# Masks as a PE bias, two heads per normalising instruction and constants behind the first loads, in a one-core attention and soft-MoE kernel

## The chip, the cores and the metric

The kernel runs on one core of a Trainium2 chip. The metric is device time in microseconds (us): the median of the runs before is 207.54 us (three runs: 206.69, 207.54 and 234.59).

The core has five engines with queues of their own, each in program order: PE (TensorE, matrix products into the eight PSUM banks), ACT (ScalarE), DVE (VectorE), POOL (GpSimd) and SP (SyncE). Here POOL issues all large loads, and SP issues the stores. Engines wait for one another through semaphores.

## The reference

Two steps follow each other. The first is attention over 8 batches, 8 heads, 576 tokens and a head size of 64. Heads 0 to 3 see the last 32 tokens ("plain"), heads 4 to 7 see every fourth of the last 128 ("dilated").

```
scores = scale * (q @ k.T);  rel = pos_q - pos_k
mask_plain = (rel >= 0) & (rel < 32)
mask_dil   = (rel >= 0) & (rel < 128) & (rel % 4 == 0)
attn = softmax(where(mask, scores, -1e9));  x = attn @ v      # x: 4608 tokens x 512
```

The second is a soft mixture of 8 experts with 4 slots each over these 4608 tokens:

```
logits = x @ phi                                  # 4608 x 32
slot_input = softmax(logits, over tokens).T @ x   # 32 x 512
slot_out[e] = relu(slot_input[e] @ w1[e]) @ w2[e] # w1: 512x1024, w2: 1024x512 per expert
out = softmax(logits, over slots) @ slot_out      # 4608 x 512
```

The output needs the sum over all tokens, so the experts can start only when the attention of the last batch is done, and the stores only when the experts are done.

## The kernel before, in words

Work is cut into 16 **halves** (`half(i)`, line 416): batch `i // 2` with its four plain heads (even `i`) or its four dilated heads (odd `i`). A half goes through these steps; the short names are those of the program's operations.

- **Loads** (line 304): k, q and v of the half, converted to bf16 on the way, into one of four staging slots. Between them POOL issues pieces of the expert weights (lines 314, 321, 328; 32 pieces in all); `W_AFTER` says how many pieces follow which half. The last six pieces of w2 are written over the staging slots, so they wait until the last half has been read out of them.
- **T** (line 426, DVE): three transposes of 32x32 blocks bring head size onto partitions.
- **SC** (lines 439 to 456, PE): scores in two rounds per half, one bank for each of the four heads (banks 0 to 3). **EX** (line 470, ACT): one exp over all four banks, which writes P to SBUF. The next round of scores needs the same banks, so it waits for EX. **MK** (line 475, DVE): P times a 0/1 mask.
- **TB** (line 497, PE) and **VE** (line 503, ACT): v transposed back to tokens on partitions, and copied out.
- **PV** (line 527, PE): per head, P times v and a column of ones, into one bank. **RC** and **NM** (lines 535, 539, DVE): reciprocal of the row sums, and the product with it. In dilated halves a rest of 64 tokens goes through PZ, RCz and NMz (lines 552, 560, 563).
- **XT** and **XE** (lines 579/585 PE, 595/598/602 ACT): x transposed. In dilated halves follow, for the batch, **LG** and **EXL** (lines 618, 626: logits and their exp), **ET** and **EE** (641, 647), **SI** (659, PE) and **SA** (667, DVE): the running sum of slot inputs.

After the last half come **RS** (line 741), the first expert product **L1** (705; banks zeroed before by DVE, line 711), its ReLU (715), transposes HT (725), the second product **L2** (757) in two halves of columns, then the output tiles **O** (788, PE), their scaling by ACT and DVE (797, 800) and twelve stores.

The order on each engine is written by a planner (`Sched`, line 51): it simulates the engines with the durations given to each `op` and takes, of what could start within 0.15 us, the operation with the smallest priority (`OFFS` and `PERIOD` give it). It also hands out PSUM banks: 0 to 3 belong to SC until the last EX, 4 to 7 go to every other PSUM user, one at a time. On POOL, constants (the identity, the masks; `const_ops`, line 353) have priority -90, and the loads of half `i` have -100 + `i`, weights -50.

Of the kernel before, what the change touches and what calls it, by code (L numbers as in the profile page):

```python
# [50 lines left out]
class Sched:  # L51
# [42 lines left out]

    def run(self, pool, late_banks, late_after):
# [13 lines left out]
        held = {b: [] for b in list(pool) + list(late_banks)}  # L109
        qfree = 0.0  # L110
# [8 lines left out]
        while True:  # L119
            best = None  # L120
            for e in self.ENG:
                cands = []
# [20 lines left out]
            for b in o.opens:
                i = min(banks, key=lambda k: (banks[k][0], k))
                _, rel = banks.pop(i)
                o.deps.update(rel)
# [25 lines left out]
def bass_dilated_sliding_attn__then__soft_moe_slots_kernel(  # L172
# [28 lines left out]
    VBK = 2 * 4 * 34  # L201
# [7 lines left out]
    o_sit = take(128)  # L209
# [688 lines left out]
```

## Time and profile before

| what | value |
|---|---|
| median of three runs | 207.54 us |
| the profiled execution's own time | 208.19 us |
| its span (first to last instruction) | 206.5 us |
| mean clock granted to PE | 0.759 |
| DVE busy / PE busy / ACT busy / POOL busy | 148.2 / 133.9 / 106.8 / 49.0 us |
| read from HBM / written to HBM | 61.93 MB / 9.44 MB |

The profiled execution took 1.69 us more than its span. Busy time is the time in which an engine worked on at least one instruction. The PE clock has two levels, 1.2 and 2.4 GHz, shown as 0.50 and 1.00; a value between them is a mean over a stretch. Bytes of loads are counted as written (bf16); twice as many are read (fp32).

### The profile page before, as it was taken

The page shows a single profiled execution, that of the slowest core. Times are in us where ns is not written, and L with a number is a line of the kernel's source. Part 1 is how long each engine was busy: PE and PEld are TensorE (multiplying, and loading weights), DVE is VectorE, ACT ScalarE, POOL GpSimd, SP SyncE. Part 2 cuts the span into 40 slices and gives each one's busy share as a digit, 9 for nine tenths or more (in the row PEclk, how much of TensorE's full clock was granted, in tenths as well). Part 3 has the DMA queues.
Part 4 walks back from the last instruction along what each step waited for, and adds up shares of the span by engine and source line. Part 5 has one row for each costly group of instructions (what it writes and reads, how often), then busy time and mean ns, then how long its engine had stood idle before and what let it go on. Part 6 is the DMA issues. An engine that isn't in the chain of part 4 may idle for free.

```text
span 206.5 us, 5220 instructions
## 1 busy us (share of the span) xinstructions
PE 133.9 (65%) x2139; PEld 96.4 (47%) x2140; DVE 148.2 (72%) x284; ACT 106.8 (52%) x167; POOL 49.0 (24%) x98
## 2 busy tenths in 40 slices
PE   0056649767794797688668489669626897988000
PEld 0045536655483576467556367447423535632000
DVE  6997698799779989999899998992673200299100
ACT  0065717845476747756677756774604140499000
POOL 7609904501504133232056000008000000000000
PEclk9999999755579567559987856966855569999655
DMA  5935999999999999999999999999999000099997
GB/s 82 206 68 102 208 210 214 210 212 211 213 211 213 213 210 212 214 210 210 212 214 208 215 212 216 210 213 195 183 193 156 3 5 0 3 300 360 417 421 330
DMA packets 19431, 40.77 MB, mean 197 GB/s; under 512 B 1744, under 2 KB 8912, under 8 KB 18640
## 3 DMA queue, kind: packets, MB, share of 16 engines
q0 software_dynamic: 15104, 30.94, 80.3%
q1 hardware_dynamic: 4304, 9.50, 12.1%
q8 instruction: 17, 0.28, 0.5%
q14 instruction: 6, 0.05, 0.1%
HBM read 61.93 MB, written 9.44 MB: 346 GB/s over the span
## 4 chain that ended last, share of the span: by engine, by line
DVE 45%; PE 33%; ACT 8%; issue 6%; DVEq 1%; ACTq 0%
DVE ar L426 16%; DVE ar L539 12%; PE ps L618 6%; PE ps L449 6%; DVE ar L475 5%; DVE fs L535 4%; PE ps L788 4%; ACT ar L470 3%; PE ps L705 3%; PE ps L757 3%; PE ps L527 3%; PE ps L585 2%; DVE ar L563 2%; ACT ar L797 2%; PE ps L497 2%
## 5 line engine op out<-in xcount | busy, mean ns | idle before, releaser
L426 DVE STREAM_TRANSPOSE ar<-ar 128x576 uint32<-128x576 uint32 x48 | 56.4, 1236 | 0.3 <-PE ps L456 0.3
L470 ACT ACTIVATE ar<-ps 128x1152 bf16<-128x1152 f32 (+1 forms) x32 | 37.9, 1186 | 21.4 <-PE ps L456 10.6
L539 DVE TENSOR_TENSOR ar<-ps,fs 96x384 bf16<-96x384 f32 (+1 forms) x64 | 31.3, 489 | 2.3
L503 ACT ACTIVATE ar<-ps 128x768 bf16<-128x768 bf16 x32 | 25.1, 816 | 6.2 <-PE ps L497 6.1
L475 DVE TENSOR_TENSOR ar<-ar 128x1152 bf16<-128x1152 bf16 (+1 forms) x32 | 24.6, 778 | 3.9 <-ACT ar L470 3.9
L527 PE MATMUL ps<-ar 128*128 128x66 bf16 x320 | 20.0, 230 | 8.5 <-DVE ar L475 3.0
L497 PE MATMUL ps<-ar 128*128 128x128 bf16 x192 | 20.2, 269 | 7.4 <-DVE ar L426 4.5
L527 PEld LDWEIGHTS ps<-ar 128*128 128x128 bf16 x320 | 17.2, 122 | 11.4 <-DVE ar L475 3.2
L497 PEld LDWEIGHTS ps<-ar 128*128 128x128 bf16 x192 | 15.9, 136 | 10.1 <-DVE ar L426 3.5
L535 DVE RECIPROCAL fs<-ps 96x6 f32<-96x6 f32 (+1 forms) x64 | 11.7, 183 | 12.3 <-PE ps L527 8.9
L449 PE MATMUL ps<-ar 32*128 32x128 bf16 x256 | 18.2, 412 | 3.3 <-ACT ar L470 2.0
L439 PE MATMUL ps<-ar 32*128 32x96 bf16 x384 | 9.3, 245 | 15.3 <-DVE ar L426 13.8
L800 DVE TENSOR_SCALAR ar<-ps,fs 128x256 f32<-128x256 f32 (+1 forms) x24 | 12.8, 611 | 7.4 <-PE ps L788 7.3
L618 PE MATMUL ps<-ar 128*128 128x288 bf16 x64 | 15.8, 422 | 3.0 <-ACT ar L602 3.0
L598 ACT ACTIVATE ar<-ps 128x1024 bf16<-128x1024 bf16 x8 | 8.2, 1025 | 16.1 <-PE ps L585 16.1
L304 POOL DMA_DIRECT2D ar<-in_k_dram x16 | 8.9, 554 | 28.8 <-DVE ar L426 28.0
L585 PE MATMUL ps<-ar 128*128 128x128 bf16 x80 | 9.5, 300 | 8.9 <-DVE ar L563 8.8
L439 PEld LDWEIGHTS ps<-ar 32*128 32x128 bf16 x384 | 6.4, 114 | 17.5 <-DVE ar L426 14.2
L321 POOL DMA_DIRECT2D ar<-in_moe_w_dram x12 | 6.4, 552 | 28.5 <-DVE ar L475 28.5
L304 POOL DMA_DIRECT2D ar<-in_v_dram x16 | 8.8, 548 | 17.8 <-DVE ar L426 13.2
L585 PEld LDWEIGHTS ps<-ar 128*128 128x128 bf16 x80 | 7.4, 137 | 10.5 <-DVE ar L563 10.5
L797 ACT ACTIVATE ar<-ps,fs 128x256 f32<-128x256 f32 (+1 forms) x24 | 12.1, 591 | 0.2
(63 smaller groups left out, 177.6 us busy)
## 6 DMA issues: line engine op xcount, KB each, us to landing
ar<-in_moe_w_dram POOLq DMA_DIRECT2D x32, 512.0 KB, 21.7
out_dram<-ar SPq DMA_DIRECT2D x6, 1024.0 KB, 9.7
ar<-in_k_dram POOLq DMA_DIRECT2D x16, 288.0 KB, 19.3
ar<-in_q_dram POOLq DMA_DIRECT2D x16, 288.0 KB, 19.4
ar<-in_v_dram POOLq DMA_DIRECT2D x16, 288.0 KB, 18.9
out_dram<-ar SPq DMA_DIRECT2D x6, 512.0 KB, 5.1
fs<-in_moe_phi_dram SPq DMA_DIRECT2D x1, 64.0 KB, 1.8
```

Of the source, the lines that this page charges most:

```text
L304: return pool.dma_start(a(o_stg + (s * 3 + j) * 1152, [[1, 1152]]), src[b, 4 * dl:4 * dl + 4].rearrange("h (p t) d -> (h p) (t d)", p=32))
L426: op(DVE, lambda j=j, o_dst=o_dst: dve.transpose(au(o_dst, [[1, 18], [18, 32]]), au(o_stg + (st * 3 + j) * 1152, [[32, 18], [1, 32]])), dv ...
L449: last = pe.matmul(pf(h, 128 * rr, [[1, 128]]), a(ok + 2 * res + par, [[8, 128]], 32 * h, 32), a(oq + 2 * res + par, [[8, 128]], 32 * h, 3 ...
L470: eo = op(ACT, lambda P=P, W=W: act.activation(a(P, [[W, 4], [1, W]]), AP(ps, 0, [[4096, 128], [512, 4], [1, W]]), ACTF.Exp, scale=SCALE), ...
L475: op(DVE, lambda P=P, W=W, msk=msk: dve.tensor_tensor(a(P, [[W, 4], [1, W]]), a(P, [[W, 4], [1, W]]), a(msk, [[0, 4], [1, W]]), AluOp.mult ...
L497: last = pe.transpose(pb(bank.idx, bb * 256 + par * 128, [[1, 128]]), src, a(o_id, [[1, 128]]))
L503: op(ACT, lambda t=t, bank=bank: act.activation(a(o_vb[vs] + 3 * t * VBK, [[34, 24], [1, 32]]), pb(bank.idx, 0, [[32, 24], [1, 32]]), ACTF ...
L527: last = pe.matmul(pf(bank.idx, 66 * t, [[1, 66]]), w, a(VB + t * VBK + 34 * h, [[136, 2], [1, 33]]), start=True, stop=True)
L535: op(DVE, lambda h=h, bank=bank, rows=rows: dve.reciprocal(f(rvo + 6 * h, [[1, NT]], 0, rows), pf(bank.idx, 32, [[66, NT]], 0, rows)), dve ...
L539: op(DVE, lambda h=h, bank=bank, rows=rows: dve.tensor_tensor(a(ox + 32 * h, [[256, NT], [128, 2], [1, 32]], 0, rows), pf(bank.idx, 0, [[6 ...
L585: last = pe.transpose(pb(bank.idx, 512 * par + 128 * (t % 4), [[1, 128]]), a(ox + 256 * t + 128 * par, [[1, 128]]), a(o_id, [[1, 128]]))
L618: last = pe.matmul(pf(bank.idx, 0, [[1, 288]]), a(o_phis + 128 * c, [[1, 128]]), a(o_xt[xt] + 576 * c + 288 * g, [[1, 288]]), start=(c == ...
```

## The change

1. **Masks as a bias.** MK is gone. Each round of SC begins with four products of the identity with a mask of 0 and -30000, 288 columns wide (plain) or 320 (dilated), which open each of the four banks; the score products add to it, and exp makes zeros of the masked places. SC now also waits for the masks that POOL and DVE build.
2. **Two heads per instruction.** PV writes two heads into two neighbouring banks, and one RC and one NM serve both: two of each per half in place of four, with twice the elements. The planner learns to hand out pairs of banks (`place`).
3. **V in natural order.** TB writes runs of 32 columns instead of 128, VE reads PSUM with a step and interleaves, so that PV's moving operand is 65 columns in a row and x keeps the order of d. The rows of w1 and phi are loaded in that order: w1 in two runs of 1024 per partition in place of one of 2048.
4. **Constants behind the first loads.** The first two weight pieces come before the constants on POOL, and `W_AFTER` is new: 0, 2, then 1 each, and 17 pieces after the last half.
5. **Smaller.** L1 uses 32 columns of weights per expert (zeros beyond the slots), so the zeroing of its banks goes; RS is behind `sit`; several estimated durations of the planner change.

```diff
-W_AFTER = [1, 1, 1, 2, 1, 1, 2, 1, 1, 2, 1, 1, 2, 1, 1, 13]
-PERIOD = 7.4
+W_AFTER = [0, 2, 1, 1, 1, 1, 1, 1, 1, 1, 1, 1, 1, 1, 1, 17]
+PERIOD = 6.9
...
+    def place(self, banks, opens, t):
+        left = dict(banks)
+        got = []
+        for b in opens:
+            best = None
+            for i in left:
+                idx = list(range(i, i + b.size))
+                if any(x not in left for x in idx):
+                    continue
+                key = (max([t] + [left[x][0] for x in idx]), i if b.size > 1 else -i)
+                if best is None or key < best[0]:
+                    best = (key, idx)
...
-            dma_in(fn, 128 * 1152 * 4, s_stg[s][j], -100.0 + i, f"ld{i}{'qkv'[j]}",
+            dma_in(fn, 128 * 1152 * 4, s_stg[s][j], (-100.0 if i < 2 else -80.0) + i, f"ld{i}{'qkv'[j]}",
...
-                a(o_w1 + e * 4096 + hf * 2048, [[1, 2048]]),
-                moe_w1[e, 256 * hf:256 * hf + 256, :].rearrange("(p two) f -> p (two f)", two=2))
+                a(o_w1 + e * 4096 + hf * 2048, [[1024, 2], [1, 1024]]),
+                moe_w1[e, 256 * hf:256 * hf + 256, :].rearrange("(c p) f -> p c f", p=128))
...
-            dma_in(fn, nb, sem("s_" + name), -50.0, name, writes=list(wr) + rd)
+            dma_in(fn, nb, sem("s_" + name), -100.0 if nw[0] < 3 else -80.0, name, writes=list(wr) + rd)
...
+            W, msk = (320, o_md + 320 * r) if dl else (288, o_mp + 96 * r)
+            for h in range(4):
+                pe.matmul(pf(h, 0, [[1, W]]), a(o_id, [[1, 128]]), a(msk, [[1, W]]),
+                          start=True, stop=False)
...
-                                start=(par == 0), stop=(par == 1))
+                                start=False, stop=(par == 1 and m % 3 == 2))
...
-            op(DVE, lambda P=P, W=W, msk=msk: dve.tensor_tensor(
-                a(P, [[W, 4], [1, W]]), a(P, [[W, 4], [1, W]]),
-                a(msk, [[0, 4], [1, W]]), AluOp.mult), dvet(2 * W),
...
-                        last = pe.transpose(pb(bank.idx, bb * 256 + par * 128, [[1, 128]]),
+                        last = pe.transpose(pb(bank.idx, bb * 256 + par * 32, [[64, 4], [1, 32]]),
...
-                a(o_vb[vs] + 3 * t * VBK, [[34, 24], [1, 32]]),
-                pb(bank.idx, 0, [[32, 24], [1, 32]]), ACTF.Copy),
+                a(o_vb[vs] + 3 * t * VBK, [[66, 12], [2, 32], [1, 2]]),
+                pb(bank.idx, 0, [[64, 12], [1, 32], [32, 2]]), ACTF.Copy),
...
-            bank = Bank(f"pv{i}{h}")
+            bank = Bank(f"pv{i}{hp}", 2)
...
-                a(ox + 32 * h, [[256, NT], [128, 2], [1, 32]], 0, rows),
-                pf(bank.idx, 0, [[66, NT], [33, 2], [1, 32]], 0, rows),
-                f(rvo + 6 * h, [[1, NT], [0, 2], [0, 32]], 0, rows), AluOp.mult),
+                a(ox + 128 * hp, [[64, 2], [256, NT], [1, 64]], 0, rows),
+                pf(bank.idx, 0, [[512, 2], [65, NT], [1, 64]], 0, rows),
+                f(rvo + 12 * hp, [[6, 2], [1, NT], [0, 64]], 0, rows), AluOp.mult),
...
-                        last = pe.matmul(pf(bank.idx, 0, [[1, 512]], 32 * j, 8),
-                                         a(o_sit + 32 * c + 8 * j, [[1, 8]]),
+                        last = pe.matmul(pf(bank.idx, 0, [[1, 512]], 32 * j, 32),
+                                         a(o_sit + 128 * c + 32 * j, [[1, 32]]),
...
-            zz = op(DVE, lambda bank=bank: dve.memset(pf(bank.idx, 0, [[1, 512]]), 0.0),
-                    dvet(512, True), T1 - .5 + g, writes=[bank], after=[last_ex[0]], name=f"Z1{g}{x}")
```

The order moves with it at three places (left-out rows are branches and repeats). The first is POOL's queue at the start of the program. Before, after the six loads of halves 0 and 1:

```order
L304 DMA ar<-in_v_dram 128x1152
...
L355 MEMSET ar 128x128
...
L362 AFFINE_SELECT ar<-ar 128x2x64 [waits c_dve,c_pool]
...
L362 AFFINE_SELECT ar<-ar 128x2x64 [waits c_pool]
...
L314 DMA ar<-in_moe_w_dram 128x2048
```

and now:

```order
L327 DMA ar<-in_v_dram 128x1152
...
L337 DMA ar<-in_moe_w_dram 128x2x1024
...
L378 MEMSET ar 128x128
...
L385 AFFINE_SELECT ar<-ar 128x2x256 [waits c_dve]
...
L385 AFFINE_SELECT ar<-ar 128x288 [waits c_pool]
...
L385 AFFINE_SELECT ar<-ar 128x2x64 [waits c_pool]
...
L327 DMA ar<-in_k_dram 128x1152
```

Eight loads instead of six stand ahead of the constants (two weight pieces more); the wait for DVE (`c_dve`) moved to an earlier select and now stands on a mask that DVE fills right behind its memsets, no longer behind five transposes.

The second place is PE's queue in an early stretch of the steady middle, around the scores of a plain half. Before:

```order
L527 MATMUL ps<-ar 128x66 [waits c_pe,c_act]
L527 MATMUL ps<-ar 128x66 x3
...
L439 MATMUL ps<-ar 128x96 [waits c_dve]
L439 MATMUL ps<-ar 128x96 x23
...
L552 MATMUL ps<-ar 128x66 [waits c_pe,c_dve]
```

and now:

```order
L460 MATMUL ps<-ar 128x288 x4
L467 MATMUL ps<-ar 128x96 x24
...
L554 MATMUL ps<-ar 128x65 [waits c_dve,c_pe]
L554 MATMUL ps<-ar 128x65 x7
...
L521 MATMUL ps<-ar 128x4x32 [waits c_act]
...
L521 MATMUL ps<-ar 128x4x32 [waits c_pe,c_dve]
```

Line 460 is the mask product, ahead of the scores in every round; line 554 is PV with two heads (8 products, or 12 in plain halves, in one group), which waits for DVE to release a pair of banks.

The third is DVE's queue in the same region. Before:

```order
L539 TENSOR_TENSOR ar<-ps,fs 96x12x32 [waits c_dve]
...
L475 TENSOR_TENSOR ar<-ar 128x1280 [waits c_act]
...
L475 TENSOR_TENSOR ar<-ar 128x1280 [waits c_act]
...
L426 STREAM_TRANSPOSE ar<-ar 128x18x32 [waits s_in00]
...
L535 RECIPROCAL fs<-ps 128x4 [waits c_pe]
...
L539 TENSOR_TENSOR ar<-ps,fs 128x8x32 [waits c_dve]
```

and now:

```order
L561 RECIPROCAL fs<-ps 96x12 [waits c_pe]
...
L565 TENSOR_TENSOR ar<-ps,fs 96x2x6x64 [waits c_dve]
...
L450 STREAM_TRANSPOSE ar<-ar 128x18x32 [waits s_in01]
...
L450 STREAM_TRANSPOSE ar<-ar 128x18x32 [waits s_in00]
...
L561 RECIPROCAL fs<-ps 96x12 [waits c_pe]
...
L565 TENSOR_TENSOR ar<-ps,fs 96x2x6x64 [waits c_dve]
```

Between the two pairs of one half (lines 561 and 565) stand two transposes of a later half; the pair of banks behind them is released only after both. The mask products of line 475 are gone.

## Rows read from the trace of the kernel before

**Rows 1.** The page: span, engines, DMA and rates by slices of 5.16 us, issues.

```profile
span 206.5 us, 5220 instructions
PE 133.9 (65%) x2139; PEld 96.4 (47%) x2140; DVE 148.2 (72%) x284; ACT 106.8 (52%) x167; POOL 49.0 (24%) x98
...
GB/s 82 206 68 102 208 210 214 210 212 211 213 211 213 213 210 212 214 210 210 212 214 208 215 212 216 210 213 195 183 193 156 3 5 0 3 300 360 417 421 330
...
q0 software_dynamic: 15104, 30.94, 80.3%
...
HBM read 61.93 MB, written 9.44 MB: 346 GB/s over the span
...
DVE 45%; PE 33%; ACT 8%; issue 6%; DVEq 1%; ACTq 0%
...
ar<-in_moe_w_dram POOLq DMA_DIRECT2D x32, 512.0 KB, 21.7
...
ar<-in_k_dram POOLq DMA_DIRECT2D x16, 288.0 KB, 19.3
```

**Rows 2.** Groups by line, shapes apart: count, busy us, mean ns, idle before.

```profile
L426 DVE STREAM_TRANSPOSE ar<-ar 128x576 uint32<-128x576 uint32 x48 | 56.4, 1236 | 0.3 <-PE ps L456 0.3
...
L539 DVE TENSOR_TENSOR ar<-ps,fs 96x384 bf16<-96x384 f32 x32 | 17.7, 554 | 1.1
...
L539 DVE TENSOR_TENSOR ar<-ps,fs 128x256 bf16<-128x256 f32 x32 | 13.6, 424 | 1.2
L475 DVE TENSOR_TENSOR ar<-ar 128x1280 bf16<-128x1280 bf16 x16 | 12.8, 812 | 2.8 <-ACT ar L470 2.8
L475 DVE TENSOR_TENSOR ar<-ar 128x1152 bf16<-128x1152 bf16 x16 | 11.7, 743 | 1.1 <-ACT ar L470 1.1
...
L535 DVE RECIPROCAL fs<-ps 96x6 f32<-96x6 f32 x32 | 6.0, 188 | 8.6 <-PE ps L527 6.9
L535 DVE RECIPROCAL fs<-ps 128x4 f32<-128x4 f32 x32 | 5.7, 178 | 3.7 <-PE ps L527 2.0
```

**Rows 3.** Windows: length, then PE, PEld, DVE, ACT, POOL busy; PEclk, DMA, GB/s.

```profile
40.00:60.00 20.00, 15.19 (x241) 11.93 (x241) 16.70 (x34) 10.78 (x17) 3.96 (x8) 0.52 1.09 211
...
100.00:120.00 20.00, 13.43 (x279) 10.30 (x275) 18.91 (x37) 13.45 (x20) 5.80 (x11) 0.85 1.09 212
```

**Rows 4.** Timeline of the start: start us, length, engine, line [idle before <- releaser].

```profile
11.39 0.67 PE L439 MATMUL ps<-ar 32*128 32x96 bf16 x24 [11.39 <-DVE ar L426]
...
15.10 1.12 POOL L362 TENSOR_SCALAR_AFFINE_SELECT ar<-ar 128x128 bf16<-128x128 bf16 x3 [6.51 <-DVE ar L379]
...
16.18 0.58 POOL L314 DMA_DIRECT2D ar<-in_moe_w_dram  x1
...
31.32 0.67 PE L439 MATMUL ps<-ar 32*128 32x96 bf16 x24 [1.00 <-DVE ar L426]
```

**Rows 5.** Timeline of the end of attention and of the experts.

```profile
139.56 0.56 PE L497 MATMUL ps<-ar 128*128 128x128 bf16 x6 [1.75 <-DVE ar L426]
...
140.06 1.07 POOL L321 DMA_DIRECT2D ar<-in_moe_w_dram  x2 [28.45 <-DVE ar L475]
...
141.18 2.10 PE L618 MATMUL ps<-ar 128*128 128x288 bf16 x8
...
148.91 1.24 ACT L470 ACTIVATE ar<-ps 128x1280 bf16<-128x1280 f32 x1 [0.26 <-PE ps L456]
...
160.44 1.34 PE L741 MATMUL ps<-ar 128*128 128x1 bf16 x36
...
168.97 1.04 PE L705 MATMUL ps<-ar 128*8 128x512 bf16 x16
...
178.61 2.13 PE L788 MATMUL ps<-ar 128*128 128x256 bf16 x13
```

**Rows 6.** PE in windows of 4 us: length, busy, PEclk, DMA share, GB/s.

```profile
92.00:96.00 4.00, 3.90 (x69) 0.82 1.09 214
96.00:100.00 4.00, 2.95 (x82) 1.00 1.11 212
```

More of the change, by code (lines that the diff above doesn't have):

```diff
@@ L108, in run @@
         banks = {b: (0.0, []) for b in pool}
-        held = {b: [] for b in list(pool) + list(late_banks)}
-        qfree = 0.0
+        qfree = 3.0
         order = []
@@ L208, in bass_dilated_sliding_attn__then__soft_moe_slots_kernel @@
     o_ek = [take(352) for _ in range(2)]
[L209 removed]
+    o_sit = take(512)
     o_mp = take(384)
@@ L373, in const_ops @@
            reads=[b_id], writes=[b_oh])
-        op(POOL, lambda: pool.memset(a(o_md, [[1, 640]]), 1.0), .4, P0, writes=[b_md])
+        op(DVE, lambda: dve.memset(a(o_md, [[1, 640]]), 0.0), .4, P0, writes=[b_md])
+        for r in range(2):
+            op(DVE, lambda r=r: dve.tensor_scalar(
+                a(o_md + 320 * r + 256, [[4, 16], [1, 4]]), a(o_oh, [[0, 16], [1, 4]]),
+                1.0, -NEG, op0=AluOp.subtract, op1=AluOp.mult), .2, P0, reads=[b_oh], rmw=[b_md])
         w = [[320, 2], [128, 2], [1, 128]]
@@ L377, in const_ops @@
         sel(o_md, w, [[0, 2], [0, 2], [-1, 128]], 31, 1, b_md)
-        for r in range(2):
-            op(DVE, lambda r=r: dve.tensor_copy(
-                a(o_md + 320 * r + 256, [[4, 16], [1, 4]]), a(o_oh, [[0, 16], [1, 4]])), .2, P0,
-               reads=[b_oh], rmw=[b_md])
         w = [[320, 2], [1, 64]]
@@ new lines, in pv_fn @@
+                for x in range(2):
+                    h = 2 * hp + x
+                    for t in range(NT):
+                        if not dl:
+                            w = a((P0 if t < 3 else P1) + 288 * h + 96 * (t % 3), [[1, 128]])
+                        else:
+                            w = a((P0 if t < 2 else P1) + 320 * h + 128 * (t % 2), [[1, 128]])
+                        last = pe.matmul(pf(bank.idx + x, 65 * t, [[1, 65]]), w,
+                                         a(VB + t * VBK + 66 * h, [[1, 65]]),
+                                         start=True, stop=True)
@@ L709, in l1_fn @@
                 return last
[L711 to L714 removed]
+            op(PE, l1_fn, pet(4, 560), T1 + 0.2 + g, reads=[b_sit] + b_w1[4 * g:4 * g + 4],
+               writes=[bank], name=f"L1{g}{x}")
             hs_ops.append(op(ACT, lambda g=g, x=x, bank=bank: act.activation(
@@ L743, in rs_fn @@
         return last
-    op(PE, rs_fn, pet(36, 60), T1 + 3, reads=[b_et, b_rm], writes=[bank], name="RS")
+    op(PE, rs_fn, pet(36, 30), T1 + 3, reads=[b_et, b_rm, b_sit], writes=[bank], name="RS")
     op(DVE, lambda bank=bank: dve.reciprocal(f(o_rinv, [[1, 36]]), pf(bank.idx, 0, [[1, 36]])),
```

151 lines of the change are left out of this document (75 added, 76 removed).

## The prediction

> **What bounds the kernel now.** I read the engines and rates first, then the durations by line, then windows of the middle, then the two ends of the timeline. The page shows no engine full over the whole span, but the chain of waits runs 45% through DVE [rows 1]. In the middle DVE works 18.91 of 20 us while PE works 13.43 and ACT 13.45 [rows 3]. The reader is to see there that DVE sets the pace of the halves. How long is one half? The first scores of half 2 start at 31.32 and the last exp of half 15 ends at 148.91 + 1.24 = 150.15 us [rows 4, 5]: 14 halves in 118.83 us, a period of 8.49 us, of which DVE works 18.91 / 20 x 8.49 = 8.03.
>
> Beside DVE stands a second bound that the busy shares hide: the loads. POOL's queue writes 30.94 MB, in most slices at 208 to 216 GB/s [rows 1]. At 211 GB/s they need 146.6 us. A half with its one weight piece is 3 x 0.295 + 0.524 = 1.41 MB (288 and 512 KB issues, [rows 1]), or 6.7 us. So the loads have only 1.8 us of slack per half, and the slices at 68 and 102 GB/s near the start, about 6 us lost, are given away: POOL's constants wait 6.51 us for a DVE copy, and the next load is issued at 16.18 [rows 1, 4].
>
> After the last exp follow 28.46 us until the first output tile (178.61), then 27.9 us to the end of the span, nearly all of it stores [rows 1, 5]. The sum below is made against the profiled execution: span 206.5, time 208.19; the median of the runs is 0.65 lower, which I leave in the range.
>
> **The change part by part.**
>
> DVE. MK goes: 2 x 0.743 = 1.49 us in a plain half, 2 x 0.812 = 1.62 in a dilated one. NM: the two shapes give (554 - 424) / (384 - 256) = 1.02 ns per element and 164 ns fixed, so 768 elements cost 0.944 and 512 cost 0.684. Four become two: 0.33 us saved in either half. RC: 5 ns per element by the same two-point reading, so about 0.22 and 0.20; 0.32 saved. Together 2.13 and 2.27, mean 2.20 us [rows 2]. DVE falls from 8.03 to 5.8 us per half. That a DVE instruction reads over two banks no row shows; the exp reads over four banks in 1.24 us for 1280 elements [rows 5], so I take nothing, and at most the saved 0.33 as the other end.
>
> PE. Eight mask products are added per half, 304 columns on average. Dear end: eight products of 288 columns took 2.10 us, 0.263 each, or 0.277 for 304 columns; 2.2 us per half. Cheap end: 16 products of 512 columns, four side by side, took 1.04 us, 0.26 per 512 columns or 0.155 for 304; 1.24 us per half [rows 5]. PE before worked 15.19 / 20 x 8.49 = 6.45 us per half where its mean clock was 0.52, and 13.43 / 20 x 8.49 = 5.70 where it was 0.85 [rows 3]. So PE comes to between 6.9 and 8.65 us per half. It was cover; now it is the fullest engine. I take the warm end plus a little, for this reason: the clock rises after stretches in which PE hardly stops (3.90 of 4 us, then 1.00 with 2.95 busy, [rows 6]), and a PE that needs 6.9 of about 7 us gives such stretches all the time.
>
> ACT works 13.45 / 20 x 8.49 = 5.7 us per half [rows 3]; its instructions keep their element counts. VE's stepped read costs between nothing and what DVE has spare; I take nothing.
>
> So the period becomes the largest of DVE 5.8, ACT 5.7, loads 6.7 and PE 6.9, plus waits between them. I take **7.1 us**.
>
> The start. The six old loads and two new weight pieces are 6 x 0.295 + 2 x 0.524 = 2.82 MB, 13.3 us of queue from about 3.2 us (slice 0 moved 82 x 5.16 = 0.42 MB, 2 us at full rate, [rows 1]), so it lasts to 16.5. The constants now need DVE only behind its memsets: the first scores at 11.39 came two transposes of 1.24 after those, so at 8.9, and I allow 1.3 for two more memsets and three small instructions. Seven selects follow, at 0.37 each (three took 1.12) or twice that: POOL's next load comes at 12.8 to 15.4 [rows 2, 4]. That is before 16.5: the hole goes. If it came back, it would cost up to 6 us of loads. The first scores wait for these constants: from 11.39 to about 13 [rows 4], 1.5 us given back. Two halves of DVE relief (4.4) against that 1.5 move the first scores of half 2 from 31.32 to about 28.
>
> The weights in shorter runs: halves of 2.3 KB rows and w2 pieces of 4 KB rows move alike (slices of 208 to 216), so 2 KB rows of w1 cost nothing. The six pieces that wait for the last staging slot (POOL waited 28.45 us and issued at 140.06, [rows 5]) are released at about 28 + 13 x 7.1 = 120 us; their 3.15 MB are not late.
>
> The experts. Out of the 28.46 us go MK (0.81), NM and RC (0.65) and RS (1.34, now behind the first product, where I charge 0.4 again) [rows 2, 5]: 26.1 remain. L1's wider weights and the zeroing cost and save nothing, since PE streams the same 512 columns and the zeroing was beside other work.
>
> **The sum.** Compute: 28 + 14 x 7.1 + 26.1 = 153.5 us to the first output tile. Loads: 3.2 + 146.6 + 2.2 = 152.0, where 2.2 is what the last four slices (195, 183, 193, 156) lose against 211; then one last pair of second products, 1.1, and hand-offs: 153.5 as well [rows 1]. Two chains that end together give the later of two, so I add 1: 154.5. Then 27.9 for the rest and 1.7 between span and time: **184 us**. Below a period of 7.1 nothing more is gained, since the loads end there; above it each 0.1 us costs 1.4.
>
> A rule that would forbid this: the Trainium skill (DMA: Bandwidth & Descriptors, Specifications) gives a core about 358 GB/s from HBM. By it 61.93 MB would end at 176 us and the kernel at about 208. The trace disagrees: a load that writes 211 GB/s of bf16 reads twice that, 422 GB/s, over some 115 us [rows 1], so the sum stays with the rows and this rule has no chance of its own.
>
> **The rivals.**
> - *PE stays at the lower level* (chance 0.27). Transposes and narrow products fill much of its time, and its clock has been 0.52 with PE at 15.19 of 20 us [rows 3], which speaks for it; against it, denser work raised the level [rows 6]. The period is then 7.4 to 8.65: at 8 us 28 + 112 + 26.1 + 29.6 = 196, at 8.65 it is 205.
> - *Pairs of banks are held too long* (0.07), the one that ends slower. Two pairs fill all four free banks, and on DVE two transposes of 1.24 us [rows 2] stand between the two NM of a half, so TB, XT, LG and the next PV wait behind a held pair; PE is in order, so the scores behind them wait too. One such wait of 2.47 us unhidden per half gives 6.9 + 2.47 = 9.4: 28 + 131.6 + 26.1 + 29.6 = 215 us. It is slower by over 2% from a period of 9.14 on. For it: the old NM released one bank every 0.74 us. Against it: DVE has 1.3 us idle per half, and PE's other groups can run meanwhile.
> - *TB's split output is slow* (0.04). If its 12 transposes took twice as long (six took 0.56, [rows 5]), PE gains 1.1 us per half: period 8.2, 199 us. The Trainium skill (PSUM — Partial Sum Buffer, Specifications) says that a non-contiguous output pattern slows matmuls significantly; no row here has such an output at short runs.
> - *The change gives more* (0.05): the clock stays up through the experts too and stores overlap the last loads: 178 to 180.
>
> **How the numbers follow.** Forecast (period up to 7.4, loads and compute end together, 182 to 188): 0.57. With the low-level rival up to 8.1 (197.5) and the smaller ones, 0.8 lie between 180 and 199, which also covers the hole at the start coming back (6 us). A measurement here tells about 2% (4.1 us) from no change: faster means below 203.4, slower above 211.7. Faster: 0.57 + 0.05 + 0.04 + 0.20 of the low-level rival = 0.86. The rest of that rival (periods from 8.55, with waits) is the same: 0.07. Slower: 0.07.
>
> **What would show it.** Right: no slice under 200 GB/s between 5 and 145 us; the last weight landing near 152; DVE below 6 us of each half; the clock mostly 1.00 in the middle; first output tile near 154. Wrong: PE gaps before lines 554, 521 or 605 released by line 565 (banks); a clock near 0.5 with PE full (low level); groups of line 521 longer than 0.9 us at the upper level (output pattern); slices near 70 GB/s at 15 us (constants late).

## The result, and the profile after

The changed kernel takes **185.97 us** (median of four runs, 185.44 to 187.06) beside 207.45 us for the kernel before on the same chip: ratio 0.898, 95% interval 0.892 to 0.904. The prediction was 184, between 180 and 199. The profiled execution took 187.06 us, 1.76 more than its span.

The page of the changed kernel: span, busy time, clock and rate in 40 slices of 4.63 us, bytes, chain by engine, and three groups that are needed below: T, TB and LG (line, shapes, count, busy us, mean ns, idle before and what ended it).

```profile
span 185.3 us, 5336 instructions
...
PE 132.0 (71%) x2268; PEld 90.2 (49%) x2268; DVE 113.9 (61%) x186; ACT 105.2 (57%) x167; POOL 51.5 (28%) x97
...
PEclk9999999999999999999999979999965799999755
...
GB/s 69 203 211 209 210 211 211 211 210 212 211 210 211 211 210 211 210 211 211 209 211 211 211 211 217 213 213 213 217 211 200 198 160 12 183 348 398 425 416 274
...
HBM read 61.93 MB, written 9.44 MB: 385 GB/s over the span
...
PE 41%; ACT 17%; DVE 16%; DMA 12%; issue 5%; ACTq 0%; DVEq 0%; POOLq 0%
...
L450 DVE STREAM_TRANSPOSE ar<-ar 128x576 uint32<-128x576 uint32 x48 | 57.5, 1245 | 9.1 <-DMA ar<-in_v_dram 3.4
...
L521 PE MATMUL ps<-ar 128*128 128x128 bf16 x192 | 17.3, 234 | 2.9 <-ACT ar L652 1.8
...
L644 PE MATMUL ps<-ar 128*128 128x288 bf16 x64 | 10.2, 307 | 1.2 <-ACT ar L628 1.2
```

Against [rows 1], DVE lost 34.3 us of work and its 45% of the chain became 16%. PE has nearly the same busy time, though it took over the masks: its clock is at the upper level in almost all slices, and its other groups take less (line 644: 10.2 us, as line 618 of the kernel before 15.8). The slices at 68 and 102 GB/s near 15 us are gone; from the second slice on none is under 198 until the last weights.

The groups of the changed lines, shapes apart (same columns):

```profile
L460 PE MATMUL ps<-ar 128*128 128x320 bf16 x64 | 13.0, 331 | 4.2 <-ACT ar L499 2.9 <-ACT ar L624 1.2
...
L460 PE MATMUL ps<-ar 128*128 128x288 bf16 x64 | 11.4, 305 | 14.4 <-DVE ar L450 12.5 <-ACT ar L499 1.9
...
L565 DVE TENSOR_TENSOR ar<-ps,fs 96x768 bf16<-96x768 f32 x16 | 15.3, 954 | 0.6
...
L565 DVE TENSOR_TENSOR ar<-ps,fs 128x512 bf16<-128x512 f32 x16 | 11.1, 692 | 0.7
...
L561 DVE RECIPROCAL fs<-ps 96x12 f32<-96x12 f32 x16 | 3.3, 205 | 14.0 <-PE ps L554 13.9
...
L561 DVE RECIPROCAL fs<-ps 128x8 f32<-128x8 f32 x16 | 3.0, 188 | 3.8 <-PE ps L554 3.7
```

NM of two heads takes 954 and 692 ns, where the prediction had 944 and 684; RC 205 and 188 for 220 and 200. So reading over two banks costs DVE 8 to 10 ns in NM beyond the line through the one-bank shapes, and nothing in RC.

Windows of the changed kernel (length, then PE, PEld, DVE, ACT, POOL busy; clock, DMA share, GB/s): one of the middle and three of the end of attention.

```profile
40.00:100.00 60.00, 51.56 (x1048) 38.03 (x1037) 50.60 (x75) 45.21 (x70) 23.86 (x42) 1.00 1.11 211
...
128.00:132.00 4.00, 3.40 (x79) 2.94 (x77) 1.66 (x4) 3.77 (x10) 0.00 (x0) 1.00 1.06 213
...
132.00:136.00 4.00, 1.49 (x31) 1.09 (x26) 2.01 (x6) 1.31 (x2) 0.00 (x0) 0.97 1.06 214
136.00:140.00 4.00, 2.60 (x19) 1.44 (x19) 0.34 (x2) 1.72 (x7) 0.00 (x0) 0.50 1.06 213
```

In the 60 us of the middle no engine is full: PE 51.56, DVE 50.60, ACT 45.21. The same window of the kernel before:

```profile
40.00:100.00 60.00, 46.12 (x801) 36.09 (x798) 54.13 (x103) 37.23 (x56) 15.57 (x30) 0.64 1.09 212
```

There DVE had 54.13 of 60 us and PE's clock stood at 0.64. The start of the changed kernel (timeline: start us, length, engine, line, [idle before <- releaser]):

```profile
10.15 2.72 POOL L385 TENSOR_SCALAR_AFFINE_SELECT ar<-ar 128x512 bf16<-128x512 bf16 x7 [2.61 <-DVE ar L434]
...
12.51 1.14 PE L460 MATMUL ps<-ar 128*128 128x288 bf16 x4 [12.51 <-DVE ar L450]
...
13.03 0.60 POOL L327 DMA_DIRECT2D ar<-in_k_dram  x1 [0.16 <-issue]
...
28.53 0.65 PE L460 MATMUL ps<-ar 128*128 128x288 bf16 x4
...
30.89 0.51 PE L521 MATMUL ps<-ar 128*128 128x128 bf16 x6 [0.51 <-DVE fs L561]
```

The constants end at 12.87 and POOL's next load goes out at 13.03 instead of 16.18 [rows 4], in time for the queue. Half 2 begins at 28.53 (31.32 before). The end of attention and the experts:

```profile
127.21 1.24 ACT L499 ACTIVATE ar<-ps 128x1280 bf16<-128x1280 f32 x1 [0.87 <-PE ps L484]
...
128.50 0.54 PE L554 MATMUL ps<-ar 128*128 128x65 bf16 x12 [0.26 <-ACT ar L499]
128.88 0.90 PE L521 MATMUL ps<-ar 128*128 128x128 bf16 x12
...
129.47 1.51 ACT L527 ACTIVATE ar<-ps 128x768 bf16<-128x768 bf16 x2 [0.23 <-PE ps L521]
...
131.03 0.41 PE L554 MATMUL ps<-ar 128*128 128x65 bf16 x8
...
136.35 2.10 PE L644 MATMUL ps<-ar 128*128 128x288 bf16 x8 [1.17 <-ACT ar L628]
...
141.84 4.82 PE L731 MATMUL ps<-ar 128*32 128x512 bf16 x48 [0.90 <-DVE ar L719]
...
150.48 6.47 PE L781 MATMUL ps<-ar 128*32 128x256 bf16 x128 [0.36 <-DVE ar L754]
156.88 5.87 PE L812 MATMUL ps<-ar 128*128 128x256 bf16 x29
```

The last exp ends at 127.21 + 1.24 = 128.45. From half 2 that is (128.45 - 28.53) / 14 = 7.14 us per half (8.49 before). Between the last exp and the first output tile lie 28.43 us, as many as before (28.46). So of the 21.1 us between the two profiled executions the start gave 2.8 and the fourteen halves 18.9; the experts gave nothing, and the stretch from there to the end took half a microsecond back.

### The profile page after: what moved, and what is told of

The parts are those of the page before. It is cut to its first block, busy times and chain, and to the rows that moved or that the text cites. A ratio compares the mean times of both kernels' runs of the same rounds, so it can differ in the third digit from the quotient of the medians.

```text
span 185.3 us, 5336 instructions
## 1 busy us (share of the span) xinstructions
PE 132.0 (71%) x2268; PEld 90.2 (49%) x2268; DVE 113.9 (61%) x186; ACT 105.2 (57%) x167; POOL 51.5 (28%) x97
## 4 chain that ended last, share of the span: by engine, by line
PE 41%; ACT 17%; DVE 16%; DMA 12%; issue 5%; ACTq 0%; DVEq 0%; POOLq 0%
DMA ar<-in_v_dram 12%; ACT ar L499 9%; PE ps L460 7%; PE ps L477 7%; PE ps L812 5%; DVE ar L450 4%; DVE ar L565 4%; PE ps L781 3%; PE ps L554 3%; PE ps L731 3%; ACT ar L527 3%; PE ps L521 2%; ACT ar L621 2%; PE ps L644 2%; PE ps L467 2%
## 5 line engine op out<-in xcount | busy, mean ns | idle before, releaser
L499 ACT ACTIVATE ar<-ps 128x1152 bf16<-128x1152 f32 (+1 forms) x32 | 37.9, 1185 | 26.9 <-PE ps L484 22.7
L460 PE MATMUL ps<-ar 128*128 128x320 bf16 (+1 forms) x128 | 24.4, 318 | 18.6 <-DVE ar L450 12.5
L565 DVE TENSOR_TENSOR ar<-ps,fs 96x768 bf16<-96x768 f32 (+1 forms) x32 | 26.3, 823 | 1.3
L460 PEld LDWEIGHTS ps<-ar 128*128 128x128 bf16 x128 | 11.2, 103 | 23.2 <-DVE ar L450 13.8
L521 PE MATMUL ps<-ar 128*128 128x128 bf16 x192 | 17.3, 234 | 2.9 <-ACT ar L652 1.8
L554 PE MATMUL ps<-ar 128*128 128x65 bf16 x320 | 15.3, 199 | 5.0 <-ACT ar L499 2.3
L561 DVE RECIPROCAL fs<-ps 96x12 f32<-96x12 f32 (+1 forms) x32 | 6.3, 196 | 17.8 <-PE ps L554 17.6
L824 DVE TENSOR_SCALAR ar<-ps,fs 128x256 f32<-128x256 f32 (+1 forms) x24 | 12.8, 609 | 7.0 <-PE ps L812 7.0
L554 PEld LDWEIGHTS ps<-ar 128*128 128x128 bf16 x320 | 12.6, 101 | 7.7 <-ACT ar L499 3.2
L521 PEld LDWEIGHTS ps<-ar 128*128 128x128 bf16 x192 | 13.1, 120 | 4.4 <-PE ps L554 1.9
L327 POOL DMA_DIRECT2D ar<-in_k_dram x16 | 9.3, 581 | 18.5 <-DVE ar L450 12.8
L327 POOL DMA_DIRECT2D ar<-in_v_dram x16 | 8.8, 551 | 17.3 <-DVE ar L450 6.8
L344 POOL DMA_DIRECT2D ar<-in_moe_w_dram x12 | 6.4, 584 | 24.1 <-DVE fs L693 24.1
L812 PE MATMUL ps<-ar 128*128 128x256 bf16 (+1 forms) x48 | 11.2, 333 | 1.3 <-DVE ar L824 0.6
L337 POOL DMA_DIRECT2D ar<-in_moe_w_dram x16 | 11.7, 737 | 0.0
L327 POOL DMA_DIRECT2D ar<-in_q_dram x16 | 8.8, 548 | 9.7 <-DVE ar L450 4.9
L644 PE MATMUL ps<-ar 128*128 128x288 bf16 x64 | 10.2, 307 | 1.2 <-ACT ar L628 1.2
```

What stands on the lines that cost most here:

```text
L327: return pool.dma_start(a(o_stg + (s * 3 + j) * 1152, [[1, 1152]]), src[b, 4 * dl:4 * dl + 4].rearrange("h (p t) d -> (h p) (t d)", p=32))
L460: pe.matmul(pf(h, 0, [[1, W]]), a(o_id, [[1, 128]]), a(msk, [[1, W]]), start=True, stop=False)
L499: eo = op(ACT, lambda P=P, W=W: act.activation(a(P, [[W, 4], [1, W]]), AP(ps, 0, [[4096, 128], [512, 4], [1, W]]), ACTF.Exp, scale=SCALE), ...
L521: last = pe.transpose(pb(bank.idx, bb * 256 + par * 32, [[64, 4], [1, 32]]), src, a(o_id, [[1, 128]]))
L554: last = pe.matmul(pf(bank.idx + x, 65 * t, [[1, 65]]), w, a(VB + t * VBK + 66 * h, [[1, 65]]), start=True, stop=True)
L565: op(DVE, lambda hp=hp, bank=bank: dve.tensor_tensor(a(ox + 128 * hp, [[64, 2], [256, NT], [1, 64]], 0, rows), pf(bank.idx, 0, [[512, 2], ...
```

## The experiments

The theory, as the prediction has it: DVE set the pace, and its relief moved the pace to a floor near 7.1 us per half that PE and the loads share. The rivals asked whether each part is needed for that, whether PE's clock or its banks hold the kernel up, and whether the loads or the experts end last. All times stand in one table; "half" is the mean period from the first exp of half 2 to the end of the last exp (8.44 before and 7.06 after by this measure). Half 2 does not start at the same time everywhere (its first exp at 29.67 in the changed kernel, at 25.42 without the mask products, at 26.78 with the old queue order). A kernel that starts early and then waits for its loads shows a long half, so the end of the last exp is to be read beside it.

| kernel | median us | ratio to before, 95% | half | last exp ends | first output tile | clock |
|---|---|---|---|---|---|---|
| changed | 185.97 | 0.892 to 0.904 | 7.06 | 128.45 | 156.88 | 0.931 |
| no mask products | 185.42 | 0.889 to 0.895 | 7.16 | 125.63 | 155.16 | 0.845 |
| single heads | 186.44 | 0.894 to 0.897 | 7.16 | 131.17 | 158.05 | 0.904 |
| mask on DVE | 188.03 | 0.902 to 0.906 | 7.42 | 131.53 | 158.13 | 0.820 |
| old queue order | 187.96 | 0.902 to 0.906 | 7.31 | 129.18 | 157.62 | 0.922 |
| before + bias | 201.24 | 0.965 to 0.972 | 7.92 | 141.97 | 171.03 | 0.866 |
| before + queue, planner | 201.04 | 0.964 to 0.973 | 8.34 | 143.87 | 172.32 | 0.762 |
| before + pairs, V order, planner | 192.75 | 0.926 to 0.934 | 7.78 | 136.63 | 162.78 | 0.834 |
| weights last | 196.12 (one run) | | 6.85 | 125.63 | 166.23 | 0.893 |
| old estimate for T | 186.68 | 0.896 to 0.904 | 7.31 | 129.04 | 155.70 | 0.932 |
| before + bias, estimate for T | 194.38 | 0.933 to 0.940 | 7.58 | 136.73 | 163.38 | 0.907 |
| both ends reordered | 187.67 | 0.897 to 0.907 | 7.60 | 133.92 | 157.42 | 0.907 |
| outputs early | 184.50 | 0.886 to 0.894 | 7.01 | 127.67 | 153.60 | 0.935 |

**1. The mask products left out**.

```
-            for h in range(4):
-                pe.matmul(pf(h, 0, [[1, W]]), a(o_id, [[1, 128]]), a(msk, [[1, W]]),
-                          start=True, stop=False)
```

> The changed kernel without its 128 mask products: the scores open their banks themselves and nothing is masked; the order on every engine is the same. Changed kernel: 186.0 us, period of a half 7.14 us, mean clock 0.93. Theory (the pace is the fullest engine's work, and the loads end just before the experts need them): PE loses 8 x 0.155 = 1.2 us per half, but the loads allow no less than 6.7 us; the period falls to 6.7 to 6.9, the attention ends 3 to 6 us earlier, the loads still end near 152, so the time is 183 to 184.5 with the first output tile near 154.5. Rival (the mask products themselves keep the clock up, and this is the gain): the mean clock falls to 0.85 or below, the period stays at 7.1 or rises, and the time is 186 or more.

The time hardly moved: 185.42 lies between the two ranges. The last exp ends 2.8 us earlier (125.63), but half 2 began 4.25 us earlier, so by the measure of the table a half is no shorter (7.16). Its middle, then T, TB and LG over the whole span, then the last products of L2:

```profile
40.00:100.00 60.00, 45.76 (x889) 36.13 (x889) 47.08 (x70) 42.30 (x67) 22.77 (x40) 0.80 1.12 211
```

```profile
L450 DVE STREAM_TRANSPOSE ar<-ar 128x576 uint32<-128x576 uint32 x48 | 58.2, 1249 | 13.5 <-DMA ar<-in_k_dram 5.8 <-DMA ar<-in_v_dram 4.1 <-PE ps L518 2.7
...
L518 PE MATMUL ps<-ar 128*128 128x128 bf16 x192 | 19.1, 251 | 3.0 <-issue 1.2 <-DVE ar L450 0.8 <-ACT ar L649 0.6
...
L641 PE MATMUL ps<-ar 128*128 128x288 bf16 x64 | 14.9, 404 | 1.2 <-ACT ar L625 1.2
```

```profile
154.18 1.05 PE L778 MATMUL ps<-ar 128*32 128x256 bf16 x16 [0.28 <-DMA ar<-in_moe_w_dram]
```

With less to do PE's clock fell from 1.00 to 0.80 of the middle, and the same groups took longer: LG 14.9 us in place of 10.2, TB 19.1 in place of 17.3. So 24.4 us of mask products cost about half a microsecond of time, which the intervals don't tell from nothing. The clock pays a part of them back. The rest is held by the loads: without the mask products the transposes wait 9.9 us for k and v (3.4 for v in the changed kernel), and the last products of L2 already wait for the last weights (0.28 us), as none do in the changed kernel. What compute gained here came up against the loads.

**2. The pairs undone**: one bank, one RC and one NM per head, the rest of the change in place.

```
-        for hp in range(2):
-            bank = Bank(f"pv{i}{hp}", 2)
+        for h in range(4):
+            bank = Bank(f"pv{i}{h}")
...
+               dvet(64 * NT, True) + .04, pr("NM") + 0.3 * h, reads=[bank, b_rv4[i % 2][h]],
...
```

> The changed kernel with its normalising undone: one head and one bank per PV, RC and NM, as before (four of each per half), all else as changed. Theory: DVE gains 0.65 us per half (5.6 to 6.3 us of 7.1), still under PE and the loads; the time is 186 to 188. Rival (pairs of banks are held too long and cost waits): single banks are released every 0.75 us, so the time falls by 2 us or more, to 184 or less.

186.44 us, the same, and as the theory expected. Holding two banks costs nothing in the middle, which was the rival on banks; but the pairs, once the masks are off DVE, also give hardly anything.

**3. The masks back on DVE**, pairs and queue order kept.

```
+            op(DVE, lambda P=P, W=W, msk=msk: dve.tensor_tensor(
+                a(P, [[W, 4], [1, W]]), a(P, [[W, 4], [1, W]]),
+                a(msk, [[0, 4], [1, W]]), AluOp.mult), dvet(2 * W),
+               pr("MK") + dr, reads=[b_md if dl else b_mp], rmw=[b_p[pi]], name=f"MK{i}{r}")
```

> The changed kernel with the mask again as a product on DVE behind the exp (32 products of 743 or 812 ns), no mask products on PE; all else as changed. Theory: DVE comes to 5.6 + 1.55 = 7.2 us per half plus its small waits, so the period is 7.4 to 7.9, the time 190 to 197, and the mean clock about 0.85. Rival (loads: what was gained is the closed hole at the start): the loads end as in the changed kernel, and the time is 185 to 188. Rival (clock): the clock falls back to 0.76 and the period to 8.2 or more, the time is 201 or more.

188.03 us, only 2.1 more than the full change and under the 190 to 197 that the theory expected; the half was in its range, the attention ends 3.1 us later, but the first output tile only 1.3 us later. Its middle:

```profile
40.00:100.00 60.00, 48.23 (x912) 38.11 (x916) 56.74 (x86) 44.25 (x69) 22.26 (x40) 0.79 1.11 211
```

DVE is full again (56.74 of 60), and a half lasts 7.42, of which DVE works 7.0. The bias moves the bound off DVE, but DVE's bound without it lies only 0.4 us per half above the other floor.

**4. The old order of the queue**: constants ahead of the loads, old `W_AFTER`.

```
-W_AFTER = [0, 2, 1, 1, 1, 1, 1, 1, 1, 1, 1, 1, 1, 1, 1, 17]
+W_AFTER = [1, 1, 1, 2, 1, 1, 2, 1, 1, 2, 1, 1, 2, 1, 1, 13]
...
-            dma_in(fn, 128 * 1152 * 4, s_stg[s][j], (-100.0 if i < 2 else -80.0) + i, f"ld{i}{'qkv'[j]}",
+            dma_in(fn, 128 * 1152 * 4, s_stg[s][j], -100.0 + i, f"ld{i}{'qkv'[j]}",
...
```

> The changed kernel with the old order of the loads and constants on POOL (6 loads, constants, then loads with the old numbers of weight pieces, 13 at the end). Theory: about 2.7 us of queue are missing before the constants and the loads stand still for 4 to 6 us near 12 to 17 us; the loads end at 156 to 158 instead of 152, later than the experts need them (now 155.8), and the time is 188 to 192. Rival (the loads have slack, compute alone sets the end): 185 to 187.

187.96 us, 2.0 more; one slice near 12 us shows 131 GB/s. The hole in the loads was worth about 2 us here: all four runs (187.49 to 188.54) lie above all four of the changed kernel (185.44 to 187.06), though the intervals of the two ratios just meet. The same holds of the masks on DVE.

**5. Each part alone on the kernel before.** The edits are the reverse of those above; the second also has the planner's new constants. The third is the changed kernel with the masks and the queue order set back, so beside the pairs it keeps the V order, the planner's constants and the smaller parts of the change (L1's columns, RS).

> The kernel before with the mask bias alone (mask products on PE, no product on DVE); one head per normalising instruction, the old queue order, the old planner constants. New theory after the first four runs (undoing any one part costs only 0.5 to 2 us of 21): the period is DVE's work per half or about 7.1 us, whichever is larger, so the parts replace one another and the first that brings DVE under 7.1 takes nearly all. Bias alone leaves DVE 8.03 - 1.55 = 6.5 us: period 7.1 to 7.3, time 187 to 191. Rival (each part is worth its share of DVE's time, 1.55 of 2.2): 192 to 196.

> The kernel before with the new order of loads and constants, PERIOD 6.9 and the new estimated durations of loads and transposes alone; mask on DVE, one head per instruction. Theory: DVE keeps 8.03 us per half, so the period stays 8.4 to 8.5; only the start gains, since the hole in the loads goes: 203 to 207. Rival (the order and the planner's constants are what gained): 195 or less.

> The changed kernel with the mask on DVE and with the old queue order: what is left of the change is two heads per normalising instruction, V in natural order and the planner's constants. Theory: DVE 8.03 - 0.65 = 7.4 us per half, period 7.4 to 7.6: time 189 to 193. Rival (share of DVE's time, 0.65 of 2.2): 200 to 203.

Alone, the bias gives 6.4 us, queue and planner 6.6, pairs with V order and planner 14.9: 28 in sum (the planner's constants are in two of them), where all together give 21.5. Undone one by one from the full change they are worth 2.1, 2.0 and 0.5. The parts replace one another: whichever two remain bring a half close to the floor. The bias alone missed its expectation by far; queue and planner gave more than their theory had (203 to 207), and the pairs lie in the range of theirs. Windows from 30 to 120 us, first before + bias, then before + queue and planner:

```profile
30.00:120.00 90.00, 73.13 (x1311) 53.46 (x1309) 67.95 (x133) 60.02 (x90) 24.42 (x46) 0.87 1.09 212
```

```profile
30.00:120.00 90.00, 68.80 (x1240) 53.06 (x1242) 83.66 (x154) 61.64 (x96) 25.45 (x48) 0.78 1.09 212
```

The second is bound by DVE (83.66 of 90). The first is bound by no engine: DVE works 75% of the time, PE 81%, and a half still lasts 7.92. My theory that a kernel freed of DVE's masks goes to the floor by itself fell.

**6. The planner's estimate for one transpose** (0.66 against 1.24 us; [rows 2] show 1.236): corrected in the kernel with the bias alone, and set back in the changed kernel.

```
-               dvet(576), pr("T") + (0.5 if j == 2 else 0.0), reads=[b_stg[st][j]],
+               1.24, pr("T") + (0.5 if j == 2 else 0.0), reads=[b_stg[st][j]],
```

> The kernel before with the bias, as in the run with the bias alone (201.2 us, period 7.92 us), and the estimated duration of a transpose at 1.24 us. Theory (order): the period falls to 7.2 to 7.5, the time to 190 to 195. Rival: 199 to 203.

> The changed kernel with one number of the planner undone: the estimated duration of a transpose, 0.66 us as before in place of 1.24 (the profile shows 1.24 to 1.25). No instruction is added or taken away, only their order changes. What is open: the bias alone gave 201.2 us although DVE works only 75% of the middle there, so something else than DVE's work sets its period of 7.9 us. Theory (the order: with the old number the planner believes DVE free 1.7 us per half too early, and queues that run in order then wait for one another): the period rises from 7.06 to 7.4 or more, the time is 190 to 197. Rival (the estimate has no effect; pairs, V's order and the queue of loads explain it): 185 to 187.5.

With the bias alone this number gives 6.9 us (201.24 to 194.38), and in the window PE goes to 76 of 90 us at a clock of 0.98:

```profile
30.00:120.00 90.00, 76.04 (x1502) 57.05 (x1502) 74.50 (x146) 67.64 (x103) 24.43 (x46) 0.98 1.09 212
```

So in that kernel the order was at fault, since nothing but the planner's order, and the banks it hands out with it, changed. How (a planner that takes a transpose for half as long as it is may put work that waits for it too early on PE) no run shows. In the changed kernel the old number costs 0.7 us, which the runs do not tell from nothing; there I had expected several. What else brings the 194.4 down to the 186.4 of the kernel with single heads (queue order, V order, the planner's other constants) I did not split.

**7. The weights moved to the end**: two pieces behind half 1, thirty behind half 15, so that the middle moves k, q and v alone.

```
+W_AFTER = [0, 2, 0, 0, 0, 0, 0, 0, 0, 0, 0, 0, 0, 0, 0, 30]
```

> The changed kernel with the weight pieces moved: 2 after half 1, the other 30 after the last half, so a half's loads alone are 0.885 MB or 4.2 us and cannot pace the halves. It ends later (30 pieces, 75 us, after the last half's loads). Theory of a pace by the loads (6.7 us per half in the changed kernel): the period between half 2 and half 15 falls to 6.5 us or less and no transpose waits for a load. Rival (PE, ACT and the waits between engines set 7.1 themselves): the period stays at 6.9 to 7.2.

```profile
L450 DVE STREAM_TRANSPOSE ar<-ar 128x576 uint32<-128x576 uint32 x48 | 57.5, 1245 | 14.5 <-PE ps L521 8.2 <-PE ps L484 6.3
```

```profile
30.00:120.00 90.00, 77.62 (x1543) 57.05 (x1543) 72.16 (x110) 69.13 (x106) 33.38 (x57) 1.00 0.99 175
```

One run. The loads have room now (175 GB/s), no transpose waits for a load any more, and a half takes 6.85 us. So with the loads out of the way compute gains 0.2 us per half, no more (the changed kernel's 3.4 us of waits for v are 0.24 per half): in this run a half has a pace of its own near 6.85, with no engine full (PE 77.62 of 90 us, DVE 72.16), and the loads' 6.7 lie just under it. Which waits between the engines make up this pace no run takes apart. The weights then come late, and the first output tile at 166.23.

**8. The two ends.** From the last exp on, the trace after shows a chain in series, so I moved TB and VE of half 15 ahead of its scores, and the output tiles of the first 256 columns ahead of the last group of L2; then the second edit alone.

```
-            op(PE, tb_fn, pet(6, 128), pr("TB") + 1.0 * t, reads=[bv, b_id], writes=[bank],
+            op(PE, tb_fn, pet(6, 128), (pr("TB") if i < NH - 1 else pr("SC") - 6.0) + 1.0 * t, reads=[bv, b_id], writes=[bank],
...
-               actt(768), pr("VE") + 1.0 * t, reads=[bank], writes=[b_vb[vs][t]], name=f"VE{i}{t}")
+               actt(768), (pr("VE") if i < NH - 1 else pr("SC") - 5.9) + 1.0 * t, reads=[bank], writes=[b_vb[vs][t]], name=f"VE{i}{t}")
...
-            out_tile(G, j, 0, 256, T2 + G)
+            out_tile(G, j, 0, 256, T1 + 24 + .1 * G)
-        store(G, 0, 256, T2 + G + .5)
+        store(G, 0, 256, T1 + 24 + .1 * G + .05)
...
-           actt(256), T1 + 25 + 20 * s, reads=[sobank[s]], writes=[b_so[s]], name=f"SO{s}")
+           actt(256), T1 + 23.9 + 20 * s, reads=[sobank[s]], writes=[b_so[s]], name=f"SO{s}")
```

> The changed kernel with two priorities moved: v of the last half is transposed before its scores (now its copy at 129.5 to 131.0 holds up PV, 2.6 us after the last exp), and the output tiles of the first 256 columns of three groups come before the last second products, so the first stores start while PE still works on the second half of columns. Theory (compute is the end by 2 to 3 us, the loads end at about 152): the first experts' product starts 1 to 2 us earlier, the first store 2 to 4 us earlier: 182 to 184.5. Rival (the loads are the end, or the stores only shift): 185 to 187.

> The changed kernel, with only the output tiles of the first 256 columns (and their stores) moved ahead of the last group of second products. Theory (compute, not the loads, sets the end, and the tail from the second products on is in series with the stores): in the changed kernel it is 185.3 - 150.48 = 34.8 us from the first second product to the end of the span; the run with both edits at the ends took 33.1. The attention is untouched here, so about 1.7 us are gained: 184 to 184.8, with first output tile near 155.5 in place of 156.88. Rival (the stores set the end whatever the order, or the stores that start earlier take rate from the last weights): 185.5 to 186.5.

Both edits: 187.67 us. The first product then starts 11.2 us after the last exp in place of 13.4, but the last exp itself comes 5.5 us later: the planner's order changed with it, and the last half alone took 11.1 us in place of 6.4. Outputs alone: 184.50 us, the lowest median of all. Its experts, PE's timeline, then its windows:

```profile
149.47 4.20 PE L781 MATMUL ps<-ar 128*32 128x256 bf16 x96 [0.36 <-issue]
153.60 1.35 PE L812 MATMUL ps<-ar 128*128 128x256 bf16 x8
155.13 0.66 PE L812 MATMUL ps<-ar 128*128 128x256 bf16 x4 [0.18 <-DVE ar L824]
155.73 2.16 PE L781 MATMUL ps<-ar 128*32 128x256 bf16 x32
```

```profile
150.00:155.00 5.00, 4.76 (x92) 3.40 (x84) 0.89 (x3) 1.44 (x4) 0.00 (x0) 1.00 0.64 87
155.00:160.00 5.00, 4.28 (x46) 2.86 (x47) 2.73 (x7) 3.02 (x9) 0.00 (x0) 1.00 0.77 250
```

The same windows of the changed kernel:

```profile
150.00:155.00 5.00, 4.41 (x104) 3.39 (x104) 0.22 (x1) 0.38 (x1) 0.00 (x0) 1.00 0.64 88
155.00:160.00 5.00, 4.70 (x50) 2.64 (x45) 2.61 (x7) 3.02 (x9) 0.00 (x0) 1.00 0.09 29
```

The queues were nearly empty between 155 and 160 us (29 GB/s); now stores fill that gap (250). From the start of L2 to the end of the span it is 182.1 - 149.47 = 32.6 us, after 34.8. The gain of some 1.5 us is expected from that; the two intervals of the ratio still touch (0.886 to 0.894, 0.892 to 0.904).

## Why the prediction was right, and where its size was off

- **DVE's relief**: right, term by term. DVE works 50.60 / 60 x 7.06 = 5.95 us per half (predicted 5.8).
- **PE**: the clock rose as argued, to 1.00 in the window from 40 to 100. The two rounds of mask products take 0.65 to 0.72 us each, so 1.3 to 1.4 per half (between the ends 1.24 and 2.2, near the warm one). But PE works only 51.56 / 60 x 7.06 = 6.07 us per half, not 6.9: I had added the masks to work measured at a clock of 0.85, and that work became cheaper too. LG fell from 15.8 us over the span to 10.2, PV from 20.0 to 15.3. So PE is the fullest engine, but does not set the pace. LG before:

```profile
L618 PE MATMUL ps<-ar 128*128 128x288 bf16 x64 | 15.8, 422 | 3.0 <-ACT ar L602 3.0
```

- **The period**: 7.14 by the prediction's own measure, 7.1 forecast. The number held, its reason only in part: it was 6.9 of PE's work plus 0.2 for waits, and the runs show 6.07 of PE's work and a pace of compute near 6.85 (one run) with no engine full, the loads' 6.7 close under it. That PE's work was put too high by about as much as the waits were put too low is luck.
- **The start**: half 2 at 28.53 (28), the next load at 13.03 (12.8 to 15.4), the hole gone. Undoing it cost 2.0 us.
- **The loads**: the last weights land near 153 us (the rate is 88 GB/s from 150 to 155, 29 after it), as worked out (152.0; by its own rows the last four slices lose 2.9 us against 211 GB/s, not 2.2, which gives 152.7). L2 ran without a wait for them.
- **From the last exp to the first output tile**: the step that was mis-sized. It forecast 26.1 and measured 28.43. The sum was made for the profiled execution, which took 187.06, so it was 3 us low: this step makes 2.3 of them, the start, the period and the stretch behind the first tile 0.5 each, less the 1 that was added for two chains. L1 starts 13.4 us behind the last exp, where the terms gave 12.9 - 0.81 - 0.65 - 1.34 = 10.1, and from L1 to the first tile it is 15.0, about 0.9 less than forecast. Two of the terms failed. Before, PV of half 15 began 0.9 us behind the last exp, LG of the last batch at 157.43 and L1 at 163.04:

```profile
151.06 1.06 PE L527 MATMUL ps<-ar 128*128 128x66 bf16 x16 [2.20 <-DVE ar L475]
...
157.43 2.08 PE L618 MATMUL ps<-ar 128*128 128x288 bf16 x8 [1.16 <-ACT ar L602]
...
163.04 5.29 PE L705 MATMUL ps<-ar 128*8 128x512 bf16 x48 [0.64 <-DVE ar L694]
```

  The first is MK's 0.81. With MK gone PV should have followed the exp at once, but it begins at 131.03, 2.6 us behind it. Its v is not transposed yet: at 128.50 PE still runs PV of half 14, at 128.88 TB of half 15, then VE on ACT (129.47 to 130.98). Banks look short there: the second pair of half 14 reads nothing that the last exp writes, and still its PV waits for that exp, which frees banks 0 to 3. But pairs alone do not bring the delay. With the old estimate for T, which keeps the pairs, and with single heads, TB of half 15 comes before the last exp, and PV follows that exp at once (0.05 and 0.06 us behind it):

```profile
129.09 0.66 PE L554 MATMUL ps<-ar 128*128 128x65 bf16 x16 [0.73 <-ACT ar L499]
```

```profile
131.23 0.66 PE L553 MATMUL ps<-ar 128*128 128x65 bf16 x16 [1.35 <-ACT ar L500]
```

  There the first output tile comes 26.7 and 26.9 us behind the last exp, near the 26.1. So these 2.5 us belong to the order that the planner wrote for the last half of this kernel, which the prediction did not look at; what in the planner led to it stays open. The second term is RS. Its 1.34 us left the stretch from the last LG to L1, but that stretch went only from 5.61 to 5.49 us: before, RS (160.44 to 161.78) ran for a good part beside the copy EE on ACT (160.64 to 161.11), for which SI, the next product, had to wait anyhow. Taking it out gained next to nothing. The low clock of the end is no part of the miss: LG takes 2.10 us at 136.35, at a clock of 0.50, where it took 1.15 at 127.09, but before it took 2.08.
- **The "+1" for two chains**: not needed in the changed kernel. The loads ended 3 to 4 us before the first output tile; compute set the end alone. But the two chains lie close: without the mask products the first tile stands at 155.16, and L2 already waits for the last weights. That the 1 offsets a part of the miss above is luck.
- **The rivals**: PE stayed at the upper level. Banks held in pairs cost nothing in the middle. The split output of TB is not slow: six transposes took 0.51 us at 30.89, and 0.56 before [rows 5]. The Trainium skill (PSUM — Partial Sum Buffer, Specifications) says that a non-contiguous output slows matmuls significantly; at runs of 32 columns this trace does not agree. In the numbers of the low level, a period of 8.1 gives 28 + 113.4 + 26.1 + 29.6 = 197.1, not 197.5, which changes nothing.

## What to carry to other kernels

When one engine sets the pace, ask first how far below it the next floor lies (loads, another engine, the waits of the order): edits do not add up past it, and here three parts worth some 28 us alone gave 21.5 together. Work given to a PE that waits can be nearly free: here the clock stayed up with it, and without it the transposes waited for loads. And follow the change to the last tile: what the middle hides comes out where the pipeline drains (an operation put off by the planner), and an instruction that runs beside a wait gives nothing when it goes.

## What the runs showed of the hardware

- 128 mask products, 24.4 us of PE, cost about 0.5 us of time, if anything: without them the granted clock of the middle fell from 1.00 to 0.80, LG's mean rose from 307 to 404 ns, and the transposes waited 9.9 us for loads in place of 3.4.
- The scores of the dilated halves (16 products on 32 rows with a strided operand) took 1.14 us at a granted clock of 0.50 (kernel before, at 53.87 us) and 1.14 at 1.00 (changed kernel, at 122.77): that group does not follow the clock, while LG does (1.15 us at 1.00, 2.10 at 0.50).
- In the changed kernel the granted clock reads 1.00 from the start, yet four mask products took 1.14 us at 12.51 and 0.65 at 28.53: early in this program the reading does not tell how fast PE runs.
- Loads that convert from fp32 to bf16 held 211 GB/s written, 422 read, over some 115 us on one core; the Trainium skill (DMA: Bandwidth & Descriptors, Specifications) has about 358 for a core, as half of what one stack gives to two. With only this core busy the trace does not show that limit.
